# A delta-rule recurrence with two feed-forward blocks: one product's queue, two merged DMAs, masking from PSUM and a two-bank evacuation

## The chip, the cores and the metric

The kernel runs on one core of one Trainium2 chip. Times are device microseconds (us) of a whole execution. The engines are named as in the profile: PE is TensorE's matmul row and PEld its weight loads, DVE is VectorE, ACT is ScalarE, POOL is GpSimd, SP is the engine that here only issues DMAs. All arithmetic is fp32 or its two-part fp32r form.

## What is computed

Four batches, 8 heads, 768 steps, head size 40. Per batch and head a 40x40 state runs through all steps; its read-out y is then fed through two feed-forward blocks.

```python
for t in range(S):
    y[:, :, t] = np.einsum('bhd,bhde->bhe', rt, state)
    Sa = np.einsum('bhde,bhe->bhd', state, at)
    state_decay = state * wt[:, :, None, :] - np.einsum('bhd,bhe->bhde', Sa, bt)
    state = state_decay + np.einsum('bhd,bhe->bhde', vt, kt)
# y as (batch, step, head * dim) = x
x  = x + relu(layernorm(x) * g_ln @ w_ch1) @ w_ch2
h  = relu(x @ w_in)                       # then a 3-tap convolution along the steps
out = (h * sigmoid(conv(h))) @ w_out
```

## The kernel before

**Chunks.** The 768 steps are cut into 24 chunks of 32. Within a chunk the recurrence is turned into matrix products, so one chunk is a chain of five products, each followed by an evacuation from PSUM, and the chunk after needs its last one. `chunk` (L552) writes the chain for both halves of the batch (half 0 and 1): `st_re` makes `reps` on PE, and ACT copies it to `re`; `st_zh` (L480) makes `zhps` from `re` and a solved triangle `tm`, and DVE multiplies it by `zmask` into `r1` (L492, four instructions per half, one for each quarter of the partitions); `st_x` (L497) makes `xps`, from which DVE scales the next state into `r1` (L516, two per half) and ACT copies `yt` (the raw y); `st_s` transposes the state (`sps`, copied to `s` by ACT); `st_xr` makes `xrps`, which ACT copies into `r1`. Throwaway bf16 products on the identity (`burn`, L129) stand ahead of some of these, three ahead of each `zhps`.

**Groups.** Two chunks are a group G (12 of them). `stage` prepares a group some 8 to 10 chunks ahead: loads, decays (the products of w, on DVE for the first four groups, then on POOL), the scaled k, b, a, their transposes (`tr`), and for each of its two chunks `inner` (L388): PE makes the 16 products `aps`, ACT writes minus them to SBUF (`pst`, L402), and DVE multiplies `pst` by `nmask`, minus a triangular mask, into the operand `l1` (L413, four instructions a chunk, eight a group). After the second chunk of the group two DMAs on SP store half of `pst` to DRAM (`pd`, L407).

**Solve.** Two groups are a quartet of four chunks, Q. `solve` (L419) loads their `pd` transposed into `sv` (L424, one buffer), inverts 128 unit triangles by 30 pairs of multiply and add (L431 and L433; on DVE for quartet 0, on POOL for the others), and stores them (`td`, L434). `load_tm` (L437) loads them back for each group, four DMAs, as `tm`, which `st_zh` needs.

**Side work.** `side` puts the following group's operands beside each chunk: `gmat` (`gps`, masked by DVE at L460), `load_stacks` (r from v at L226, l from ks at L229), and `yout` (L561), which transposes a quarter of an earlier quartet's `yt` (`yps`), multiplies it on DVE by the decays `gtok` (L575, one instruction for each half), and stores each half with a DMA of its own (L578) to `xs`, a DRAM tile for each batch and half of the steps. `load_g` (L370) loads `gtok` once a quartet with four DMAs, one for each batch (L372).

**PSUM.** Three pools of two buffers: `pm`, one bank a buffer (`reps`, `zhps`, `sps`, `xrps` in turn), `px`, two banks a buffer (`xps`), and `pside`, one bank a buffer (`tr`, `tre`, `aps`, `gps`, `yps`).

**Order.** The program gives each instruction a priority by chunk (`at`), and a list scheduler places every engine's instructions in one fixed order from these and its own model of durations; on the chip each engine keeps that order. Waits follow from the tiles.

**After the recurrence** the feed-forward blocks run over eight blocks of 384 steps; `load` (L883) reads a block of `xs`. Their code is not touched but for that index.

## Time and profile before

| | us |
|---|---|
| runs before, median (three runs, 940.84 to 951.85) | 951.68 |
| the profiled execution | 944.43 |
| its span, first to last instruction | 942.7 |
| busy in the span: PE, DVE, ACT, POOL | 820.1, 679.3, 513.7, 273.6 |

The span has three parts: the start-up up to the first `zhps` product, the 24 chunks, and the feed-forward blocks. A busy share says which engine has much to do, not which wait ends last; on this kernel the latter is read from the gaps in PE and DVE within a chunk. Times in the rows count from the span's start.

### The profile page before, as it was taken

Reading aid. Unit: us, or ns where it says so; the run is one execution under the profiler, and the core shown is the slowest. Engines: PE = TensorE matmul, PEld = TensorE weight load, DVE = VectorE, ACT = ScalarE, POOL = GpSimd, SP = SyncE. Lnnn points to the kernel's source line nnn. Section 1 sums busy time; section 2 is a strip of 40 time slices with the busy share of each in tenths; the row PEclk is TensorE's granted clock in tenths of the full one; section 3 lists DMA queues with packets and bytes.
Section 4 is the critical chain, followed back from the end, with each engine's and each line's share of the span. In section 5 each row is a group of like instructions: output and inputs, shape, how many; then the busy total and the mean of one; then the engine's idle time right before and its main releaser. Section 6 shows DMA issues by size and latency. Waiting matters only on the chain.

```text
span 942.7 us, 24879 instructions
## 1 busy us (share of the span) xinstructions
PE 820.1 (87%) x9959; PEld 721.8 (77%) x9959; DVE 679.3 (72%) x1646; ACT 513.7 (54%) x1166; POOL 273.6 (29%) x498
## 2 busy tenths in 40 slices
PE   0575587797989999979998898999999999999996
PEld 0454465675767777757767877999999999999996
DVE  8879848677667786779888989785649482756356
ACT  6267255854766766545544357564438362746354
POOL 9403268359339448085112222000000000000000
PEclk9867798997999999998999989999999999999999
DMA  5997784684697585683745541101010000000000
GB/s 153 206 235 193 185 170 97 170 186 98 170 166 182 149 164 110 133 158 91 145 109 153 142 114 50 36 1 36 1 36 15 22 15 2 29 1 15 15 15 32
DMA packets 218544, 94.21 MB, mean 100 GB/s; under 512 B 176860, under 2 KB 207924, under 8 KB 218420
## 3 DMA queue, kind: packets, MB, share of 16 engines
q1 hardware_dynamic: 217524, 90.24, 40.8%
q0 software_dynamic: 896, 2.30, 1.1%
q8 instruction: 80, 1.31, 0.6%
q14 instruction: 44, 0.36, 0.1%
HBM read 63.78 MB, written 28.72 MB: 98 GB/s over the span
## 4 chain that ended last, share of the span: by engine, by line
PE 49%; DVE 20%; DMA 8%; ACT 5%; POOL 4%; issue 3%; SPq 2%; DVEq 0%; ACTq 0%; POOLq 0%
PE ups L946 17%; PE acc L956 9%; PE accb L956 8%; DVE r L492 4%; PE xps L505 3%; DVE l L413 3%; PE tps L924 2%; PE tr L323 2%; POOL sv L433 2%; POOL svt L431 1%; PE xrps L544 1%; PE aps L397 1%; DMA x<-xs 1%; DVE r L460 1%; PE reps L474 1%
## 5 line engine op out<-in xcount | busy, mean ns | idle before, releaser
L492 DVE TENSOR_TENSOR r<-zhps,zmask 32x288 f32<-32x288 f32 x192 | 87.2, 454 | 33.7 <-PE zhps L487 28.1
L964 DVE SCALAR_TENSOR_TENSOR rl<-ups,rh 128x384 fp32r<-128x384 f32 x80 | 44.6, 557 | 82.6 <-ACT rh L963 82.4
L963 ACT ACTIVATE rh<-ups 128x384 fp32r<-128x384 f32 x80 | 39.0, 490 | 105.7 <-PE ups L946 105.1
L505 PE MATMUL xps<-r,l 128*40 128x72 f32 x1536 | 82.0, 239 | 13.2 <-DVE r L492 12.3
L505 PEld LDWEIGHTS xps<-r,l 128*40 128x40 f32 x1536 | 62.7, 122 | 32.8 <-DVE r L492 24.9
L433 POOL TENSOR_TENSOR sv<-sv,svt 128x30 f32<-128x30 f32 (+9 forms) x150 | 83.3, 555 | 9.4
L946 PE MATMUL ups<-xh,w1h 128*128 128x384 f32 x240 | 81.2, 339 | 1.7 <-DVE rl L964 1.3
L431 POOL TENSOR_TENSOR svt<-sv 128x30 f32<-128x30 f32 (+9 forms) x150 | 77.9, 520 | 9.2
L946 PE MATMUL ups<-xh,w1l 128*128 128x384 f32 x240 | 80.6, 336 | 0.0
L413 DVE TENSOR_TENSOR l<-pst,nmask 32x256 f32<-32x256 f32 x96 | 58.3, 607 | 24.5 <-ACT pst L402 23.4
L956 PE MATMUL acc<-w2h,rh 128*128 128x320 f32 x240 | 71.6, 310 | 1.7 <-ACT rh L963 1.7
L956 PE MATMUL acc<-w2l,rh 128*128 128x320 f32 x240 | 71.4, 307 | 0.0
L946 PE MATMUL ups<-xh,w3l 128*128 128x384 f32 x192 | 65.1, 341 | 0.3 <-POOL w3l L806 0.3
L134 ACT COPY yt<-xps 40x256 f32<-40x256 f32 x96 | 35.2, 367 | 55.0 <-DVE r L516 50.5
L946 PE MATMUL ups<-xh,w3h 128*128 128x384 f32 x192 | 64.4, 342 | 0.6 <-ACT h L988 0.4
L956 PE MATMUL accb<-w4h,ph 128*128 128x320 f32 x192 | 59.1, 313 | 0.0
L956 PE MATMUL accb<-w4l,ph 128*128 128x320 f32 x192 | 58.7, 309 | 0.0
L956 PE MATMUL acc<-w2h,rl 128*128 128x320 f32 x240 | 49.8, 312 | 6.0 <-DVE rl L964 6.0
L956 PE MATMUL accb<-w4h,pl 128*128 128x320 f32 x192 | 53.4, 311 | 0.6 <-DVE pl L1010 0.6
L946 PE MATMUL ups<-xl,w1h 128*128 128x384 f32 x160 | 53.5, 335 | 0.0
L999 DVE SCALAR_TENSOR_TENSOR c<-h,taps,c 128x256 f32<-128x256 f32 (+1 forms) x88 | 43.9, 508 | 12.8 <-ACT c L997 12.6
L516 DVE TENSOR_TENSOR r<-xps,ge 40x320 f32<-40x320 f32 x96 | 46.7, 486 | 8.3 <-PE xps L505 6.1
(190 smaller groups left out, 2219.4 us busy)
## 6 DMA issues: line engine op xcount, KB each, us to landing
l<-ks SPq DMA_DIRECT2D x44, 160.0 KB, 3.5
raw<-in_moe_w_ch_dram SPq DMA_DIRECT2D x17, 320.0 KB, 3.4
ks<-p_b SPq DMA_DIRECT2D x12, 416.0 KB, 3.3
ks<-p_k SPq DMA_DIRECT2D x12, 416.0 KB, 4.0
ld_w<-in_w_dram SPq DMA_DIRECT2D x24, 160.0 KB, 3.3
ld_k<-in_k_dram SPq DMA_DIRECT2D x24, 160.0 KB, 4.2
ld_a<-in_a_dram SPq DMA_DIRECT2D x24, 160.0 KB, 3.7
ld_b<-in_b_dram SPq DMA_DIRECT2D x24, 160.0 KB, 3.8
```

The source lines that it names most:

```text
L134: return self.nc.scalar.copy(out, in_).ins
L413: nc.vector.tensor_tensor(out=lv[v0:v0 + C, :, :, y, c, 32 * half:32 * half + C], in0=pst[64 * y:64 * y + C, :, :, half], in1=self.nmask[6 ...
L431: eng.tensor_tensor(out=tmp, in0=sv[:, 0:u, u:u + 1].to_broadcast([128, u, m]), in1=sv[:, u:u + 1, u + 1:C].to_broadcast([128, u, m]), op= ...
L433: last = eng.tensor_tensor(out=sv[:, 0:u, u + 1:C], in0=sv[:, 0:u, u + 1:C], in1=tmp, op=ALU.add)
L492: nc.vector.tensor_tensor(out=r1[z0:z0 + 32, :, x, MO[y]:MO[y] + 72], in0=ps[32 * q:32 * q + 32], in1=self.zmask[32 * q:32 * q + 32].rearr ...
L505: nc.tensor.matmul(ps[x0:x0 + D, j >> 2, o:o + 72], lhsT=l2[:, i, :], rhs=r1[:, j, MO[y]:MO[y] + 72], start=True, stop=True)
L516: last = nc.vector.tensor_tensor(out=r2[X0:X0 + D, :, :, VO[y]:VO[y] + D], in0=pv[x0:x0 + D, :, :, v:v + D], in1=ge[X0:X0 + D, :, :, y, c: ...
L946: self.mm = self.nc.tensor.matmul(ps, lhsT=l, rhs=r, start=(i == 0), stop=(i == len(passes) - 1)).ins
L956: self.mm = self.nc.tensor.matmul(acc[n][:, 0:DM], lhsT=l, rhs=r, start=(f == 0 and i == 0), stop=(f == nf - 1 and i == 2)).ins
L963: nc.scalar.activation(rh, ps, AF.Relu)
L964: nc.vector.scalar_tensor_tensor(out=rl, in0=ps, scalar=0.0, in1=rh, op0=ALU.max, op1=ALU.subtract)
L999: nc.vector.scalar_tensor_tensor(out=c, in0=h(1), scalar=w(1), in1=c, op0=ALU.mult, op1=ALU.add)
```

## The change

- The two halves swap their partitions (`XR0`, `VR0`, `ZR0`), so that half 0 stands first in `yt`; batch indices follow.
- `nmask` goes. L413 now reads the product in PSUM and multiplies by `mask` instead of reading `pst` and multiplying by `nmask`. ACT still writes `pst`, for the store.
- The `pd` stores are issued by ACT instead of SP.
- `gtok` is loaded with one DMA a quartet instead of four.
- `yout` multiplies both halves in one instruction and stores both with one DMA. For that `xs` becomes one DRAM tile for each half of the steps that holds all batches.
- `zhps` moves from `pm` to `px`. Its products for the two row groups (x = 0, 1) go to partitions 0 to 63 of two banks instead of to the two halves of the partitions of one bank, and two instructions of 576 columns a half replace four of 288 at L492.

```diff
     def st_zh(self, n, half, re):
-        r1 = self.r1[n % 2][half].rearrange("p (k x) m -> p k x m", x=2)
-        ps = self.psm("zhps")[:, 0:288].rearrange("p (k m) -> p k m", k=4)
+        r1 = self.r1[n % 2][half].rearrange("p (k x) m -> p x k m", x=2)
+        ps = self.psx("zhps")[0:64, :, 0:288].rearrange("p x (k m) -> p x k m", k=4)
...
-            nc.tensor.matmul(ps[64 * x:64 * x + 64, k, :], lhsT=tm[64 * x:64 * x + 64, k, half, :],
+            nc.tensor.matmul(ps[:, x, k, :], lhsT=tm[64 * x:64 * x + 64, k, half, :],
...
-        for q in range(4):
-            x, y = q >> 1, q & 1
+        for y in range(2):
             nc.vector.tensor_tensor(
-                out=r1[z0:z0 + 32, :, x, MO[y]:MO[y] + 72], in0=ps[32 * q:32 * q + 32],
-                in1=self.zmask[32 * q:32 * q + 32].rearrange("p (o t) -> p o t", o=1).to_broadcast([C, 4, 72]),
+                out=r1[z0:z0 + 32, :, :, MO[y]:MO[y] + 72], in0=ps[32 * y:32 * y + 32],
+                in1=self.zmask[32 * y:32 * y + 32].rearrange("p (o q t) -> p o q t", o=1, q=1).to_broadcast([C, 2, 4, 72]),
                 op=ALU.mult)
```

```diff
     def inner(self, n):
...
-            for y in range(2):
-                nc.sync.dma_start(out=self.pd[n // 4][:, 64 * g + 32 * y:64 * g + 32 * y + 32],
-                                  in_=self.pst[64 * y + 32:64 * y + 64].rearrange("s x c k f t -> s (x c k f) t"))
+            self.pd_store(self.pd[n // 4][:, 64 * g:64 * g + 64])
...
+        pv = ps.rearrange("p (k x) (f t) -> p x k f t", x=2, f=2)
...
-                    in0=pst[64 * y:64 * y + C, :, :, half],
-                    in1=self.nmask[64 * y:64 * y + C].rearrange("p (o q t) -> p o q t", o=1, q=1).to_broadcast(
+                    in0=pv[64 * y:64 * y + C, :, :, half],
+                    in1=self.mask[64 * y:64 * y + C].rearrange("p (o q t) -> p o q t", o=1, q=1).to_broadcast(
...
+    def pd_store(self, pd):
+        for y in range(2):
+            self.nc.scalar.dma_start(out=pd[:, 32 * y:32 * y + 32],
+                                     in_=self.pst[64 * y + 32:64 * y + 64].rearrange("s x c k f t -> s (x c k f) t"))
```

```diff
     def load_g(self, Q):
-        for b in range(B):
-            self.nc.sync.dma_start(out=self.gtok[:, b], in_=self.gs[Q][b].rearrange("h t e -> t h e"))
+        self.nc.sync.dma_start(out=self.gtok.rearrange("t b h e -> t (b h) e"),
+                               in_=self.gs[Q].rearrange("b h t e -> t (b h) e"))
...
     def yout(self, Q, part):
-        for half in range(2):
-            ys = self.tile([128, 4, D], f"ys_{half}", YB, self.yp)
...
+        ys = self.tile([128, 2, 4, D], "ys", YB, self.yp)
...
+        nc.sync.dma_start(out=self.xs[Q // 3][b01::2, t0:t0 + 128, D * h0:D * h0 + 4 * D].rearrange("b t e -> t b e"),
+                          in_=ys.rearrange("p b h e -> p b (h e)"))
```

## Rows read from the trace of the kernel before

**Rows 1.** Engines' busy time by stretch (instructions in brackets), granted TensorE clock, DMA share

```profile
0.00:113.00 113.00, 56.58 (x598) 44.07 (x599) 93.93 (x259) 61.07 (x109) 47.81 (x75) 0.79 0.79 198
113.00:188.00 75.00, 59.39 (x1166) 46.78 (x1166) 48.56 (x86) 45.28 (x100) 42.70 (x91) 0.89 0.64 144
188.00:259.00 71.00, 63.30 (x1208) 49.50 (x1209) 50.87 (x99) 42.60 (x97) 43.20 (x88) 0.89 0.66 151
...
502.00:943.00 441.00, 419.25 (x2612) 409.92 (x2611) 299.50 (x799) 221.22 (x534) 23.07 (x28) 0.99 0.13 36
```

**Rows 2.** DVE's timeline in chunk 14: start, us, instructions merged

```profile
356.16 6.32 DVE L413 TENSOR_TENSOR l<-pst,nmask 32x256 f32<-32x256 f32 x8 [2.17 <-ACT pst L402]
362.51 0.56 DVE L575 TENSOR_TENSOR ys<-yps,gtok 128x160 f32<-128x160 f32 x2
363.10 3.85 DVE L492 TENSOR_TENSOR r<-zhps,zmask 32x288 f32<-32x288 f32 x8
...
368.29 2.00 DVE L516 TENSOR_TENSOR r<-xps,ge 40x320 f32<-40x320 f32 x4
```

**Rows 3.** PE's timeline in chunk 14

```profile
357.73 0.71 PE L474 MATMUL reps<-r,l 128*32 128x72 f32 x32
...
360.73 0.72 PE L487 MATMUL zhps<-re,tm 64*64 64x72 f32 x16
```

**Rows 4.** Groups of instructions by line: busy us, mean ns | idle before

```profile
L413 DVE TENSOR_TENSOR l<-pst,nmask 32x256 f32<-32x256 f32 x96 | 58.3, 607 | 24.5 <-ACT pst L402 23.4
```

**Rows 5.** Durations of single instructions, min/median/max ns, by tile

```profile
L492 DVE TENSOR_TENSOR r<-zhps,zmask x192: 446/453/465, 115.0 to 500.5; 32x288 f32<-32x288 f32 x192
...
L516 DVE TENSOR_TENSOR r<-xps,ge x96: 450/484/495, 120.5 to 502.6; 40x320 f32<-40x320 f32 x96
...
L413 DVE TENSOR_TENSOR l<-pst,nmask x96: 404/416/4919, 40.3 to 394.6; 32x256 f32<-32x256 f32 x96
L407 SPq DMA_DIRECT2D pd<-pst x24: 319/422/1616, 46.0 to 392.3; - x24
```

**Rows 6.** DVE's timeline around chunk 6

```profile
216.28 9.73 DVE L413 TENSOR_TENSOR l<-pst,nmask 32x256 f32<-32x256 f32 x8 [3.58 <-ACT pst L402]
```

**Rows 7.** PE's timeline around chunk 6

```profile
220.32 0.72 PE L487 MATMUL zhps<-re,tm 64*64 64x72 f32 x16
...
227.12 0.46 PE L505 MATMUL xps<-r,l 128*40 128x72 f32 x2 [5.74 <-DVE r L492]
```

**Rows 8.** DVE's timeline in chunk 2

```profile
142.40 10.35 DVE L413 TENSOR_TENSOR l<-pst,nmask 32x256 f32<-32x256 f32 x8 [3.69 <-ACT pst L402]
```

**Rows 9.** PE's timeline in chunk 2

```profile
146.76 0.72 PE L487 MATMUL zhps<-re,tm 64*64 64x72 f32 x16
154.19 1.10 PE L323 MATMUL tr<-ident,p_a 128*104 128x128 f32 x4 [6.71 <-DVE r L460]
```

**Rows 10.** Waits over the whole span: us in total, times, longest

```profile
ACT yt L134 <- DVE r L516: 50.5, 16, 13.6
...
PEld tr L323 <- DVE r L460: 8.8, 3, 6.9
PE zhps L487 <- DMA tm<-td: 8.6, 5, 3.9
```

**Rows 11.** PE's timeline, the first `zhps` of chunks 4 and 8

```profile
188.51 0.71 PE L487 MATMUL zhps<-re,tm 64*64 64x72 f32 x4 [3.10 <-DMA tm<-td]
...
260.44 0.68 PE L487 MATMUL zhps<-re,tm 64*64 64x72 f32 x14 [1.22 <-DMA tm<-td]
```

**Rows 12.** SP's timeline between two solves

```profile
326.89 2.08 SPq L407 DMA_DIRECT2D pd<-pst  x2
...
331.21 4.38 SPq L372 DMA_DIRECT2D gtok<-gs  x4
335.64 0.75 SPq L424 DMA_DIRECT2D sv<-pd  x1
```

**Rows 13.** Issue of the `sv` load, min/median/max ns

```profile
L424 SPq DMA_DIRECT2D sv<-pd x6: 387/496/752, 59.1 to 396.2; - x6
```

More of the change, by code (lines that the diff above doesn't have):

```diff
@@ L20 @@
 NQ = NCH // 4
-XR0 = (64, 0)
-VR0 = (0, 64)
-ZR0 = (32, 96)
+XR0 = (0, 64)
+VR0 = (64, 0)
+ZR0 = (96, 32)
 SLOT = 168
@@ L89, in __init__ @@
         self.kb = T([128, 16, 2, 64], "kb", ep)
-        self.mask, self.nmask = T([128, C], "mask"), T([128, C], "nmask")
+        self.mask = T([128, C], "mask")
         self.zmask = T([128, 72], "zmask")
@@ L120, in psm, with psx @@
         return self.burn(self.pm.tile([128, 512], F32, tag="m", name=name), BURN.get(name, 0))
-    def psx(self):
-        ps = self.px.tile([128, 2, 512], F32, tag="x", name="xps")
-        self.burn(ps[:, 0], BURN.get("xps", 0))
+    def psx(self, name="xps"):
+        ps = self.px.tile([128, 2, 512], F32, tag="x", name=name)
+        self.burn(ps[:, 0], BURN.get(name, 0))
         return ps
@@ L166, in constants @@
         P.memset(self.kb[96:128], 0.0)
-        V.tensor_scalar(self.nmask, self.mask, -1.0, None, op0=ALU.mult)
         self.at(-16.5)
@@ L572, in yout @@
         pv = ps[:, 0:416].rearrange("p (h m) -> p h m", h=4)
-        for half in range(2):
-            ys = self.tile([128, 4, D], f"ys_{half}", YB, self.yp)
-            self.last_out = nc.vector.tensor_tensor(
-                out=ys, in0=pv[:, :, XR0[half]:XR0[half] + D], in1=self.gtok[:, 2 * half + b01, h0:h0 + 4],
-                op=ALU.mult).ins
-            nc.sync.dma_start(out=self.xs[2 * half + b01][Q // 3][t0:t0 + 128, D * h0:D * h0 + 4 * D],
-                              in_=ys.rearrange("p h e -> p (h e)"))
+        ys = self.tile([128, 2, 4, D], "ys", YB, self.yp)
+        self.last_out = nc.vector.tensor_tensor(
+            out=ys, in0=bass.AP(tensor=pv.tensor, offset=pv.offset, ap=[pv.ap[0], [64, 2], pv.ap[1], [1, D]]),
+            in1=self.gtok[:, b01::2, h0:h0 + 4], op=ALU.mult).ins
+        nc.sync.dma_start(out=self.xs[Q // 3][b01::2, t0:t0 + 128, D * h0:D * h0 + 4 * D].rearrange("b t e -> t b e"),
+                          in_=ys.rearrange("p b h e -> p b (h e)"))
     def at(self, t):
@@ L1167, in sequential @@
             for i in range(B):
-                nc.sync.dma_start(out=xs[i][half][bass.ds(t0, step), :].rearrange("t (h e) -> h t e", h=H),
+                nc.sync.dma_start(out=xs[half][i][bass.ds(t0, step), :].rearrange("t (h e) -> h t e", h=H),
                                   in_=y[H * i:H * i + H])
@@ L1181, in run_kernel @@
         excess = cp.tile([128, 2 * NG], F32, name="excess")
-        xs = [[dp.tile([TG, DM], F32, name=f"xs_{i}{j}") for j in range(2)] for i in range(B)]
+        xs = [dp.tile([B, TG, DM], F32, name=f"xs_{j}") for j in range(2)]
         early = ExitStack()
```

10 lines of the change are left out of this document (5 added, 5 removed).

## The prediction

> **What bounds the kernel now.** I read the stretches first. [rows 1] cut the span at the first `zhps` (113 us) and after the last chunk (502 us): a start-up of 113, a recurrence of 389, and 441 for the feed-forward blocks, where PE is busy 419 of 441. The change touches nothing in the last part but the shape of `xs`, so whatever it does must be found in the first 502 us, and above all in the 389 of the chunks, 16.2 us a chunk. In the two stretches of [rows 1] between 113 and 259 PE is busy 59.4 of 75 and 63.3 of 71: there is room, but no engine is full.
>
> Second, one chunk on DVE and PE. In chunk 14 [rows 2] DVE runs without a pause from 356.16 to 370.3: masking (L413) 6.32, then the eight `zhps` evacuations 3.85, then a mask of side work, then the state (L516) 2.00. The `zhps` product of half 0 was ready at 360.73 + 0.72 = 361.45 [rows 3], and its evacuation began at 363.10, behind the masking. So here DVE's queue sets the pace, and the masking is what stands in the way.
>
> Third, the masking itself. L413's median is 416 ns, its longest 4919 [rows 5]; 96 of them take 58.3 us [rows 4], where 96 medians would be 39.9. The surplus of 18.4 sits in a few groups of eight, which should take 8 x 0.416 = 3.3: 10.35 in chunk 2 [rows 8], 9.73 around chunk 6 [rows 6], 6.32 in chunk 14 [rows 2], that is 7.0, 6.4 and 3.0, and 2.0 elsewhere. The instructions that read PSUM and a mask in SBUF never show this: L492 446 to 465, L516 450 to 495 over the whole recurrence [rows 5]. L413 is the one of them with both sources in SBUF. In chunk 6 the harm is plain: the second `zhps` ended at 221.04, and PE's next stall of 5.74 us ended at 227.12 with L492 [rows 7]. In chunk 2 PE stood 6.71 us, from 147.48 to 154.19, before a `tr` that needed the bank masked at L460, and L460 was queued behind L413 [rows 8, 9].
>
> Fourth, what stands beside the chunks. The `tm` of every fourth chunk comes from the solve: PE waited 3.10 us for it in chunk 4 and 1.22 in chunk 8 [rows 11], 8.6 in five waits in all [rows 10]. So the loop pst, `pd`, `sv`, solve, `td`, `tm` is as long as four chunks to within a few us: it is late next wherever a chunk gets shorter.
>
> **The change part by part.** The sum is made against the profiled execution, 944.4 us (span 942.7).
>
> *Masking from PSUM.* No row shows 256 columns from PSUM. L492 takes 453 for 288 and L516 484 for 320 [rows 5], about 1 ns a column, so 256 take about 0.42 us: as fast as L413's median, but without the stalls. DVE saves 96 x (0.607 - 0.422) = 17.8 us. On the path I count what PE or the evacuation waited: 6.7 in chunk 2, 5.7 in chunk 6 and 363.10 - 361.45 = 1.6 in chunk 14, together 14. Bounds: 0, if the solve gives all back, and 17.8.
>
> It does not spare the wait for `pst`. L413 waited 23.4 us for ACT's `pst` [rows 4], and would seem to need only the product now. But ACT's `yt` copies waited 50.5 us for DVE's L516 [rows 10], though both only read `xps`: readers of one PSUM tile on two engines are put one behind the other, and `pst` is written first. [...]
>
> *The price of that.* A bank of `aps` is now free only after its four masks (1.7 us) instead of after `pst`, and the two chunks of a group hold both `pside` banks together for up to 3.4 us, in which no `tr`, `gps` or `yps` can start. The cover is the chain, which uses the other pools. The nearest row is L460, which holds a bank in the same way: `tr` waited 8.8 us for it, 6.9 of it once [rows 10], in chunk 2 behind the stalled masking, so 1.9 without a stall. Eight groups fall in the recurrence: 0 to 8 x 3.4 = 27. A static order made with that holding in view will move side work away; I take 0.4 each, 3 us, near the row's 1.9.
>
> *z and H in two instructions.* An instruction of 576 columns should cost 0.453 + 288 x 0.97 ns = 0.73 us, against 0.91 for two of 288 [rows 5]. Eight with their gaps take 3.85 [rows 2]; four will take about 3.85 - 4 x 0.17 - 4 x 0.03 = 3.05. So 0.8 us a chunk, 19 over 24 chunks, is the upper bound. The first `xps` products used to start after the first two of four evacuations and can no longer, so of half 0's share little reaches the path. I take 0.6 a chunk, 14 us. Lower bound 0.
>
> *The products for it.* The two row groups now write the same partitions in two banks. The trace never shows two row groups on one set of columns. Bounds: 16 records took 0.72 us in two column groups and 32 in 0.71 in four [rows 3]; less about 0.22 for the first, 33 and 16 ns a record, so four groups run twice as fast as two and one group would need 66: (0.72 - 0.22) x 2 + 0.22 = 1.22, or 0.5 more a half, 48 x 0.5 = 24 us. Lower bound 0, which I take: row groups are separate parts of the array as column groups are, and every row here has groups running beside each other. [...]
>
> `zhps` in `px` has to wait for the readers of the last chunk's `xps`, L516 and the `yt` copies; L516 ends at 370.3 [rows 2], while the next `zhps` is due a chunk of 16.2 us after 360.73 [rows 3], near 377, so nothing.
>
> *pd on ACT's queue.* An issue takes 0.42 us in the median and 0.59 in the mean (14.2 for 24), 0.32 at least [rows 5]. 16 of the 24 fall in the recurrence: 16 x 0.42 = 6.7, to 9.4, of ACT's time right after `pst`, with `re`, `r` and `s` copies queued behind it. About a third should meet a copy that is waiting: 3 us. SP loses the same issues: in [rows 12] two of them took 2.08 directly on the way to the next solve.
>
> *gtok in one DMA, y in one store.* Four `gtok` issues took 4.38 us just ahead of an `sv` load [rows 12]; that `sv` load has as many short pieces as a merged one and is issued in 0.50 [rows 13]. SP gets free 3.9 us earlier, but the bytes are the same and `sv` follows them, so I take half, 2, and with `pd` 1 more: 3 us less on a solve loop where this order occurs. `yout`: 0.56 for two [rows 2] becomes about 0.48; 24 x 0.08 = 2, off the path. The loss of `nmask` is one small instruction.
>
> **The sum.** Gains of the chunks: 14 + 14 = 28. But the solve paces too. Up to chunk 4 the chunks gain 6.7 + 4 x 0.6 = 9.1, while PE already waits 3.10 there: only what the solve itself gains, about 2 from SP and a POOL that DVE's masking no longer disturbs, comes through. At chunk 8 the same: 2 more, of 8.1. From there on PE does not wait as much, the earlier masking starts the third solve earlier, and the chunks' own gain can come through: 3 for chunks 8 to 11, 4 for 12 to 15 with the stall of chunk 14, 2.4 each for 16 to 19 and 20 to 23. Together 2 + 2 + 3 + 4 + 2.4 + 2.4 = 15.8. Less 3 for ACT's issues and 3 for the held banks: 9.8. 944.4 - 9.8 = 934.6. The profiled execution is 7.3 below the median of the runs shown, and these spread over 11 us; the same share, 1.04%, off 951.68 gives 941.8. I put the median of the changed kernel between the two, at 938.0, which is 1.4% under the median shown.
>
> **The rivals.**
>
> *The chunks' gain comes through whole* (chance 0.27). For it: the masking's stalls are direct waits of PE, and once chunk 6 is quick the third solve starts sooner; the solve loop contains SP issues of 2.08 and 4.38 that go. Also PE's granted clock is 0.89 from 113 to 259 [rows 1], where the stalls are, so a steadier PE may get more of its higher level. Against: 3.10 and 1.22 us of waiting for `tm`. Time: 944.4 - 28 = 916 if the 3 from SP pay for ACT's issues, 919 with the held banks.
>
> *All is given back* (0.20). The solve loop is unchanged, each chunk 4Q waits for it, and the issues on ACT and held banks take the rest. Time: 944.4 - 2.4 (after the last solve) + 3 = 945.
>
> *Row groups on one set of columns do not run together* (0.10, the other side). The point from which it decides is a `zhps` group of 16 records longer than 0.72 + 15.8 / 48 = 1.05 us; at 1.22 it costs 24, and since `zhps` lies on the chain all of it counts: 934.6 + 24 = 959, slower than the profiled execution by 1.5%.
>
> *Held banks stop PE for their full length* (0.06): 27 in place of 3, 958.6.
>
> **How the numbers follow.** The forecast, with its own range of 928 to 944, has 0.37. A measurement of this kernel tells about 2% from no change: faster means below 932.6, slower above 970.7. Faster takes most of the first rival and a little of the forecast's lower end: 0.27. Slower needs two of the costs at once, or an order of the scheduler that nobody foresees: 0.10. The rest, 0.63, is no change. The range reaches from the first rival, 916, to the last two, 959, leaving out a tenth on each side.
>
> **What would show it.** L413's longest under 0.5 us and its 96 near 40: right on the stalls; still several us long: wrong. L492 96 instructions of 0.73 each, four in about 3.05. A `zhps` group still 0.72, else the third rival. PE's wait for `tm` should grow in chunks 4 and 8; if it does not and the last chunk ends before 485, the first rival holds. PE waiting for L413 or for `pst` with `tr`, `gps` or `yps` shows held banks. ACT copies late behind an issue of `pd` by more than 0.5 us each make the 3 us too small. What I can't see is the new static order, which can move any of this by several us.

## The result, and the profile after

The changed kernel takes 957.84 us (median of four, 957.3 to 958.2) where the kernel before, run beside it, takes 949.73: a ratio of 1.014, with a 95% interval of 1.010 to 1.018. A second comparison on another chip gives 953.86 against 941.9, again 1.014 (1.009 to 1.020). The ratios are estimates from all fast runs of both kernels and not quotients of these medians, which differ by 8.1 us, and on the second chip by 12.0. So it is slower by 8 to 13 us. That is inside the 2% that the forecast called no change and inside its range, but the forecast had its middle on the other side.

The spans of the two profiled executions differ by 13.1 us (955.8 and 942.7). The table cuts them at rows of PE's timeline: the first `aps` product, the first `zhps` of chunks 0, 16, 20 and 23, and the end. The third line is a second profile of the changed kernel.

| us | to first aps | to zhps 0 | chunks 0-16 | 16-20 | 20-23 | rest | span |
|---|---|---|---|---|---|---|---|
| before | 35.2 | 77.7 | 280.8 | 65.3 | 37.3 | 446.4 | 942.7 |
| after | 37.9 | 85.5 | 267.1 | 77.1 | 36.2 | 452.1 | 955.8 |
| after again | 34.8 | 84.9 | 266.7 | 74.3 | 36.5 | 450.1 | 947.3 |

The chunks up to the sixteenth did gain, 13.7 us. Three other places lost: 7.8 in the start-up behind the first `aps`, 11.8 in the four chunks 16 to 19, and 5.7 in the rest. In the second profile the gain is 14.1 and the losses are 7.2, 9.0 and 3.7. The 2.7 ahead of the first `aps` differ from one execution of the same kernel to the next.

First the parts that came out as written. Durations of single instructions of the kernel after (min/median/max ns, then first and last start), to be held against [rows 5]:

```profile
L411 DVE TENSOR_TENSOR l<-aps,mask x96: 405/418/423, 42.8 to 398.1; 32x256 f32<-32x256 f32 x96
...
L495 DVE TENSOR_TENSOR r<-zhps,zmask x96: 746/750/755, 125.0 to 506.8; 32x576 f32<-32x576 f32 x96
...
L420 ACTq DMA_DIRECT2D pd<-pst x24: 308/346/584, 45.2 to 394.8; - x24
```

The masking has no stall left: the longest of 96 is 423 ns, where it was 4919, and its 96 take 40.0 us for 58.3 [rows 4]. Four evacuations of z and H take 3.06 us for the eight's 3.85 [rows 2], as this row of DVE's timeline in chunk 2 shows:

```profile
152.99 3.06 DVE L495 TENSOR_TENSOR r<-zhps,zmask 32x576 f32<-32x576 f32 x4
```

Then the waits of the kernel after over the whole span (us in total, times, longest), beside [rows 10]:

```profile
PE zhps L491 <- DMA tm<-td: 15.9, 5, 9.7
...
PE tr L322 <- DVE l L411: 8.7, 5, 2.6
...
PE tre L322 <- DVE l L411: 8.2, 3, 4.7
...
PE ups L948 <- ACT w3h L806: 4.2, 3, 3.1
```

PE's wait for `tm` has nearly doubled, from 8.6. The two rows of L411 are the held banks: 16.9 us in which a transpose waited for the masking to free its bank. The last row is in the feed-forward part, where the kernel before waits 0.2 us.

The 9.7 us stand at one place, the first `zhps` of chunk 20, on PE's timeline:

```profile
467.56 0.71 PE L491 MATMUL zhps<-re,tm 64*64 64x72 f32 x4 [9.70 <-DMA tm<-td]
```

Its `reps` came at 454.4, two microseconds earlier than before's 456.4, but before went on with `zhps` at 459.0. What was late is the fifth of POOL's solves, that of quartet 5 for chunks 20 to 23; it is called the fifth solve here, and its way from `pd` to `tm` the fifth loop. SP's timeline where it begins, after and then before:

```profile
394.39 0.47 SPq L370 DMA_DIRECT2D gtok<-gs  x1
394.96 5.46 SPq L217 DMA_DIRECT2D ld_v<-in_v_dram  x1
400.52 1.03 SPq L225 DMA_DIRECT2D r<-in_v_dram  x2
...
404.87 1.26 SPq L428 DMA_DIRECT2D sv<-pd  x1
```

```profile
391.80 0.90 SPq L407 DMA_DIRECT2D pd<-pst  x2
396.16 0.39 SPq L424 DMA_DIRECT2D sv<-pd  x1
396.65 3.38 SPq L578 DMA_DIRECT2D xs<-ys  x2
400.08 3.55 SPq L372 DMA_DIRECT2D gtok<-gs  x4
```

Before, `sv` leaves 0.1 us after its `pd` landed at 396.1, and `gtok` follows it. After, `pd` lands at 399.7, and `sv` stands behind `gtok` and eight other loads: it leaves 5.1 us later, at 404.87. Once the solve runs, it takes 50.6 us on POOL (48.7 before), the longest of the five that POOL does, because POOL's fixed order, in both kernels, puts a weight subtraction between its pairs that waits for ACT (6.3 us here, 8.2 before):

```profile
438.07 0.62 POOL L437 TENSOR_TENSOR sv<-sv,svt 128x228 f32<-128x228 f32 x1
445.01 0.86 POOL L808 TENSOR_TENSOR w1l<-v,w1h 128x320 fp32r<-128x320 f32 x1 [6.32 <-ACT w1h L806]
```

In the second profile of the changed kernel this solve takes 47.6 us, less than before's 48.7, and chunk 20 still stands 11.8 us between `reps` and `zhps` (13.1 in the first profile, 2.6 before). So the solve's own length is not what was lost.

In the start-up `td` is late too, though its place in SP's queue is the old one. After, the solve on DVE ends at 109.7 and `td` leaves 5.0 us later, behind five other DMAs. Before, it ends at 103.5 and `td` leaves at 104.17, behind the same five, which had left by then. The first of them, `bd`, stores `blk`, a product of POOL, and that came later: 72.1 us behind the first `aps`, 64.7 before. The solve itself ended 3.4 us later, counted in the same way. The timelines of POOL and SP after, and then before:

```profile
109.62 0.35 POOL L235 TENSOR_TENSOR blk<-t 128x80 f32<-128x80 f32 x1
...
109.99 0.33 SPq L246 DMA_DIRECT2D bd<-blk  x1
111.54 0.58 SPq L248 DMA_DIRECT2D pre<-bd  x1
112.54 1.29 SPq L366 DMA_DIRECT2D gs<-p_g  x2
113.92 0.65 SPq L217 DMA_DIRECT2D ld_w<-in_w_dram  x1
114.66 0.54 SPq L438 DMA_DIRECT2D td<-sv  x1
```

```profile
99.47 0.35 POOL L236 TENSOR_TENSOR blk<-t 128x80 f32<-128x80 f32 x1
...
99.85 0.34 SPq L247 DMA_DIRECT2D bd<-blk  x1
...
104.17 0.64 SPq L434 DMA_DIRECT2D td<-sv  x1
```

### The profile page after: what moved, and what is told of

The parts are those of the page before. It is cut to its first block, busy times and chain, and to the rows that moved or that the text cites. A ratio compares the mean times of both kernels' runs of the same rounds, so it can differ in the third digit from the quotient of the medians.

```text
span 955.8 us, 24666 instructions
## 1 busy us (share of the span) xinstructions
PE 810.3 (85%) x9959; PEld 721.0 (75%) x9959; DVE 654.9 (69%) x1525; ACT 514.9 (54%) x1166; POOL 277.7 (29%) x498
## 4 chain that ended last, share of the span: by engine, by line
PE 47%; DVE 14%; DMA 8%; POOL 7%; ACT 5%; issue 4%; SPq 3%; DVEq 0%; ACTq 0%; POOLq 0%
PE ups L948 17%; PE acc L958 9%; PE accb L958 8%; POOL svt L435 3%; POOL sv L437 3%; DVE r L495 2%; PE xps L508 2%; DMA x<-xs 2%; PE tps L926 2%; DMA gtok<-gs 1%; PE xrps L547 1%; SPq L217 1%; PE zhps L491 1%; DVE r L519 1%; DVE p_k L286 1%
## 5 line engine op out<-in xcount | busy, mean ns | idle before, releaser
L495 DVE TENSOR_TENSOR r<-zhps,zmask 32x576 f32<-32x576 f32 x96 | 72.0, 750 | 38.7 <-PE zhps L491 36.9
L965 ACT ACTIVATE rh<-ups 128x384 fp32r<-128x384 f32 x80 | 39.1, 490 | 107.6 <-PE ups L948 107.3
L435 POOL TENSOR_TENSOR svt<-sv 128x30 f32<-128x30 f32 (+9 forms) x150 | 80.2, 535 | 9.9
L437 POOL TENSOR_TENSOR sv<-sv,svt 128x30 f32<-128x30 f32 (+9 forms) x150 | 80.2, 535 | 9.6
L508 PE MATMUL xps<-r,l 128*40 128x72 f32 x1536 | 64.9, 244 | 18.6 <-issue 11.4
L508 PEld LDWEIGHTS xps<-r,l 128*40 128x40 f32 x1536 | 57.4, 128 | 25.8 <-issue 12.9
L134 ACT COPY yt<-xps 40x256 f32<-40x256 f32 x96 | 35.2, 367 | 68.5 <-DVE r L519 67.4
L411 DVE TENSOR_TENSOR l<-aps,mask 32x256 f32<-32x256 f32 x96 | 40.0, 417 | 34.5 <-ACT pst L401 33.1
L491 PE MATMUL zhps<-re,tm 64*64 64x72 f32 x768 | 37.9, 240 | 19.5 <-DMA tm<-td 15.9
L519 DVE TENSOR_TENSOR r<-xps,ge 40x320 f32<-40x320 f32 x96 | 46.8, 487 | 10.1 <-PE xps L508 8.5
```

The lines of the kernel that those rows point to most:

```text
L134: return self.nc.scalar.copy(out, in_).ins
L411: nc.vector.tensor_tensor(out=lv[v0:v0 + C, :, :, y, c, 32 * half:32 * half + C], in0=pv[64 * y:64 * y + C, :, :, half], in1=self.mask[64 ...
L435: eng.tensor_tensor(out=tmp, in0=sv[:, 0:u, u:u + 1].to_broadcast([128, u, m]), in1=sv[:, u:u + 1, u + 1:C].to_broadcast([128, u, m]), op= ...
L437: last = eng.tensor_tensor(out=sv[:, 0:u, u + 1:C], in0=sv[:, 0:u, u + 1:C], in1=tmp, op=ALU.add)
L491: nc.tensor.matmul(ps[:, x, k, :], lhsT=tm[64 * x:64 * x + 64, k, half, :], rhs=re[64 * x:64 * x + 64, k, :], start=True, stop=True)
L495: nc.vector.tensor_tensor(out=r1[z0:z0 + 32, :, :, MO[y]:MO[y] + 72], in0=ps[32 * y:32 * y + 32], in1=self.zmask[32 * y:32 * y + 32].rearr ...
```

## The experiments

All ratios are to the kernel before, run beside each on the same chip. The tables give stretches as above, from each run's profile.

### One part taken back at a time

Theories: Q, the fifth `sv` is late because it stands behind `gtok`; H, the banks held by the masking delay the fifth `pd`; S, the loss is spread by the new order; Z, `zhps` in `px` waits for readers.

**gtok behind sv.** `load_g` is ordered behind the last `sv` load on SP.

```diff
-            self.load_g(n // 4)
+            with self.tc.issue_after(self.sv_load):
+                self.load_g(n // 4)
```

> The changed kernel with one order forced: each gtok load is issued after the latest sv load (they share SP's queue). Theory Q (the one-piece gtok load fills SP's queue ahead of the fifth sv load, so the fifth solve comes late): PE's 9.70 us wait for tm at the first zhps of chunk 20 falls under 2 us, the fifth sv load is issued at its pd's landing instead of 5 us later, and the time falls by 7 to 9 us, to about 949. Theory H (the masks hold both pside banks and so delay the solve's input): the wait stays above 6 us and the time within 3 us of 957.8. Theory S (any new order moves the start and the tail by several us): the time may fall or rise by up to 10 us, with the chunk 20 wait not the place of it.

**gtok in four loads again.**

```diff
-        self.nc.sync.dma_start(out=self.gtok.rearrange("t b h e -> t (b h) e"), ...)
+        for b in range(B):
+            self.nc.sync.dma_start(out=self.gtok[:, b], in_=self.gs[Q][b].rearrange("h t e -> t h e"))
```

> The changed kernel with gtok loaded by four DMAs again; the order still has the fifth sv load seven places behind it. Theory Q in its first form (one big DMA blocks, four small ones do not): the issue right behind gtok falls from 5.46 us to under 2, the chunk 20 wait to under 5, time about 952. Theory Q in its second form (the bytes ahead of sv count, not the number of issues): four issues take 3.5 to 4.4 us together as in the kernel before, the wait stays at 8 to 10 us, time 956 to 959. Theory H: 957.8 within 3.

**Masks from SBUF again.**

```diff
-                    in0=pv[64 * y:64 * y + C, :, :, half],
-                    in1=self.mask[64 * y:64 * y + C]...
+                    in0=pst[64 * y:64 * y + C, :, :, half],
+                    in1=self.nmask[64 * y:64 * y + C]...
```

> The changed kernel with L413's masking from pst and nmask in SBUF again, everything else as changed. Theory H: the held banks were the loss; tre and tr no longer wait for masks, time 945 to 950. [...] Theory S: anything between 945 and 965.

**z and H in one bank again**, four instructions a half.

```diff
-        ps = self.psx("zhps")[0:64, :, 0:288].rearrange("p x (k m) -> p x k m", k=4)
+        ps = self.psm("zhps")[:, 0:288].rearrange("p (k m) -> p k m", k=4)
...
-        for y in range(2):
+        for q in range(4):
+            x, y = q >> 1, q & 1
```

> The changed kernel with zhps in one bank of pm and four evacuations of 288 a half again. In its order the fifth sv load stands six places ahead of gtok. Theory Q: no wait over 2 us at chunk 20, which gives 8 back; the chunks lose 0.6 each, 14 over the recurrence where nothing else paces; time 952 to 960, with the first zhps still after 120 us. Theory Z (moving zhps into px cost the time, since its products wait for the copies of yt): time 944 to 950 and xps no longer waiting.

| | ratio (95%) | first aps to zhps 0 | 0-16 | 16-20 | rest |
|---|---|---|---|---|---|
| after | 1.014 (1.010-1.018) | 85.5 | 267.1 | 77.1 | 452.1 |
| gtok behind sv | 1.011 (1.002-1.020) | 80.4 | 268.8 | 77.5 | 450.0 |
| gtok in four | 1.015 (1.005-1.024) | 85.8 | 268.0 | 76.2 | 452.6 |
| masks from SBUF | 1.015 (1.006-1.023) | 79.3 | 276.2 | 74.6 | 450.8 |
| z, H in one bank | 1.015 (1.005-1.024) | 85.6 | 277.8 | 74.4 | 448.9 |

Taking back the masking or the evacuation costs the chunks 0 to 16 9.1 and 10.7 us. But no single undoing brings back the 65.3 of chunks 16 to 19. With `gtok` behind `sv`, `sv` left at once, but `pd` itself landed 14.8 us after chunk 16's `zhps` instead of 9.2: Q alone is not it. With `gtok` in four, `sv` left 6.8 us after its `pd`: the number of DMAs is not it. With the masks from SBUF the banks are free again and the wait stays, so H alone is not it either. Z finds little: the throwaway products ahead of `zhps` wait 1.2 us in all for the copies of `yt` in the changed kernel, and at most 4.0 in any version here. What remains is S, that the order as a whole is another one, and that is not yet a mechanism.

### Each part alone, and the solve halved

Theory L: the loop of `pd`, `sv`, solve, `td` and `tm` takes the chunks' gain back. M: the start-up is lost by the masking from PSUM. Rivals are named in the expectations.

**Masks from PSUM alone**, on the kernel before.

```diff
-                    in0=pst[64 * y:64 * y + C, :, :, half],
-                    in1=self.nmask[64 * y:64 * y + C]...
+                    in0=pv[64 * y:64 * y + C, :, :, half],
+                    in1=self.mask[64 * y:64 * y + C]...
```

> Kernel before with one part alone: masks read PSUM and nmask goes. Theory M (the lost start-up comes with masking from PSUM): first zhps near 123 us as in the changed kernel (112.9 before), chunks 0 to 16 about 9 us quicker than before's 280.8, so near 272, and the time about that of the kernel before or up to 8 us more, ratio 1.000 to 1.008. Rival P (the start-up was lost by pd on ACT's queue or the one gtok load): first zhps near 113, and then the time is below before's by up to 5 us. Theory L (the loop of the solve takes the chunks' gain back at chunk 20): PE waits 5 to 10 us for tm at chunk 20 (0 before).

**z and H in two banks alone**, the `st_zh` of the change on the kernel before.

```diff
-        ps = self.psm("zhps")[:, 0:288].rearrange("p (k m) -> p k m", k=4)
+        ps = self.psx("zhps")[0:64, :, 0:288].rearrange("p x (k m) -> p x k m", k=4)
```

> Kernel before with one part alone: zhps in two banks of px, two evacuations of 576 columns a half. Start-up untouched: first zhps near 113. Chunks 0 to 16 about 10 us quicker than 280.8, near 271. Theory L (solve loop): PE waits at chunk 20 for tm, 5 us or more, and the time is below before's by no more than 5 us, ratio 0.995 to 1.000. Rival K (the loss at chunk 20 comes from the masks' holding of pside or from the store and load order of the other parts): no wait at chunk 20, and the whole 10 us stay, ratio 0.989.

**Half of solves 1 to 5 left out**, in the kernel before and in the changed one. Both leave out every second pair of multiply and add on POOL, so they compute something else and serve for their times only.

```diff
-        for u in range(C - 2, 0, -1):
+        for u in range(C - 2, 0, -1 if eng is nc.vector else -2):
```

> Kernel before, but solves 1 to 5 (on POOL) do only every second pair of multiply and add, so td holds other numbers; each solve is some 20 us shorter. This is the base for the next run. By theory L the kernel before waits 8.6 us for tm in all, and these go: 5 to 12 us less than before. Rival N (the solve is hidden in the kernel before): within 3 us of it.

> Changed kernel with the same half of solves 1 to 5 left out. Theory L (solve loop takes the chunks' gain back): the wait of 9.7 us at chunk 20 is gone, so it is quicker than the changed kernel by 12 us or more, and compared with the kernel before with the same half left out the stretch from first zhps to the end of chunk 23 is 12 to 18 us shorter, the start-up 10 us longer: the two within 5 us of each other, before side by side 13 apart. Rival K (chunk 20 waits for something else): the wait stays within 3 us and so does the distance of 13 us to the base.

**pd on ACT's queue alone.**

```diff
-                nc.sync.dma_start(out=self.pd[n // 4]...
+                nc.scalar.dma_start(out=self.pd[n // 4]...
```

> Kernel before with one part alone: pd is issued by ACT. By the prediction's term 3 us are lost on ACT and 1 gained on SP: ratio 1.000 to 1.004, no wait at chunk 20. Rival O (any change of the order of SP around the fifth solve starts it late, whatever the part): sv of the fifth solve leaves 5 us or more after its pd landed, PE waits 8 us or more at chunk 20, ratio 1.008 to 1.015.

**gtok in one load and y in one store alone**, with the swap of the halves that they need.

```diff
-        for half in range(2):
-            ys = self.tile([128, 4, D], f"ys_{half}", YB, self.yp)
+        ys = self.tile([128, 2, 4, D], "ys", YB, self.yp)
...
-        for b in range(B):
-            self.nc.sync.dma_start(out=self.gtok[:, b], ...)
+        self.nc.sync.dma_start(out=self.gtok.rearrange("t b h e -> t (b h) e"), ...)
```

> Kernel before with gtok in one load, y of both halves in one multiply and one store (with the swap of the halves), all else as before. By the prediction's term at most 3 us less. Rival O (any other order on SP loses the fifth loop): sv leaves late behind gtok, 16 to 20 takes 73 to 78 (65.3 before), ratio 1.008 to 1.015. If the tail after the chunks is 440 or more (436 before), the 5 us that the changed kernel loses there come from the merged y store.

| | ratio (95%) | first aps to zhps 0 | 0-16 | 16-20 | rest |
|---|---|---|---|---|---|
| before | | 77.7 | 280.8 | 65.3 | 446.4 |
| masks alone | 1.015 (1.007-1.024) | 81.8 | 271.7 | 78.0 | 447.7 |
| z, H alone | 1.022 (1.015-1.030) | 79.8 | 278.4 | 77.8 | 447.5 |
| pd on ACT alone | 1.010 (1.005-1.014) | 78.9 | 273.7 | 76.3 | 445.0 |
| gtok and y alone | 1.023 (1.017-1.029) | 78.9 | 276.1 | 79.5 | 453.3 |
| before, half solve | 0.989 (0.985-0.993) | 80.1 | 266.6 | 65.4 | 446.3 |
| after, half solve | 0.986 (0.978-0.994) | 86.0 | 250.3 | 67.2 | 450.2 |

Four quite different edits lose the same 11 to 14 us in chunks 16 to 19, and together they lose no more. So it is not something that a part costs; it is something that the order of the kernel before has and the orders of these four lack. The granted clock does not go with it: in these chunks it was 0.92 before, 0.88 after, and 0.93 with `pd` on ACT alone, which lost 11.0. The row of `pd` on ACT alone, PE's timeline at chunk 20:

```profile
469.61 0.74 PE L487 MATMUL zhps<-re,tm 64*64 64x72 f32 x4 [6.15 <-DMA tm<-td]
```

The times missed what was expected of three of the four: the masks alone 1.015 for at most 1.008, z and H alone 1.022 for at most 1.000, `gtok` and y alone 1.023 for at most 1.015. `pd` on ACT came out in its rival's range, but not by the rival's way: `sv` left 1.2 us after its `pd` had landed, where 5 or more were named.

The half solve says what takes the gain. The kernel before gets 1.1% quicker by it; the changed kernel, 1.4% above before with a whole solve, ends 1.4% below, and the chunks 16 to 19 are back at 67.2. In this execution chunk 20 goes from `reps` to `zhps` without a stop:

```profile
436.21 0.71 PE L478 MATMUL reps<-r,l 128*32 128x72 f32 x32
436.85 0.72 PE L491 MATMUL zhps<-re,tm 64*64 64x72 f32 x16
```

PE waits for `tm` no longer at all (15.9 us with the whole solve; the base falls from 8.6 to 4.1). With the solve out of the way the chunks from 0 to 23 take 355.8 us, 15.3 below the base's 371.1, where with the whole solve they take 380.4, 3.0 below before's 383.4. So the loop of the solve takes back 12.3 of 15.3. That is theory L. The half solve gives the base more than a shorter loop, though: its 96 masks, both of whose sources lie in SBUF, take 48.8 us for 58.3, while POOL has less to do. So 15.3 may be less than the parts are worth without a loop. The two were expected within 5 us of each other; the changed kernel came out 4.6 below.

M holds in part: the masks alone lose 4.1 us behind the first `aps`, and taking them back from the changed kernel returns 6.2; the other parts alone lose 1.2 to 2.1, no more than the kernel before with half the solve (2.4). The late `blk` goes with the masks: where the start-up's masks read SBUF, it ended 64.7 to 66.5 us behind the first `aps` in all eleven profiles, and where they read PSUM 70.5 to 73.3 in seven of eight. The eighth is `gtok` behind `sv`: there `blk` ended at 58.3, `td` left as the solve ended, and 5.1 us came back with the masks still in PSUM. So in the first profile 4.3 of the 7.8 us are `td` held behind a `bd` that waits for POOL, and most of the others the solve's later end; why the masks put POOL and the solve late was not moved alone.

The rest of the loss, 5.7 us (3.7 in the second profile), goes with the y of both halves in one store: `gtok` and y alone have 453.3 us behind the chunks; the twelve profiles with the merged store have 447.3 to 453.3, the seven without it 444.8 to 447.7. `gtok` in four did not mend it (452.6). In `gtok` and y alone PE's `ups` waits 4.2 us for `w3h`, as in the changed kernel. Which of SP's loads holds `w3h` up was not tried. Part of the loss can be PE's clock: behind the chunks PE is busy 424.3 us at a granted clock of 0.99 before, 425.9 at 0.98 in the changed kernel, and 428.7 at 0.97 in `gtok` and y alone. But in the second profile of the changed kernel it is 423.3 at 0.99, and 3.7 are lost all the same.

### What in the fifth loop is late

Theory O: SP's fixed order puts `sv`, `td` and `tm` of the fifth solve behind other DMAs.

**The w1l subtractions kept on DVE until chunk 21** (`SUBN = 21` for 18), so that POOL's fifth solve waits for nothing; on the kernel before, on the changed kernel, and on the changed kernel with the start-up's masks from SBUF.

> Kernel before, with the subtractions that make w1l kept on DVE until chunk 21 (POOL takes them from chunk 18), so that the fifth solve on POOL does not wait for ACT's w1h (8.2 us in the kernel before). Base for the next run. The kernel before does not wait at chunk 20, so by theory L (solve loop) this brings it little: within 3 us, ratio 0.997 to 1.003. Rival T (the subtractions on DVE cost as much as they free): 3 to 8 us slower.

> Changed kernel with the same edit. Theory L: the fifth solve falls from 50.5 us to about 40, PE's wait at chunk 20 from 13 us between reps and zhps to 2 to 5, and the time by 8 to 11 against the changed kernel, so to a ratio of 1.002 to 1.006. Rival G (the chunk-20 loss comes from the late store and load of the fifth pd and not from the length of the solve): the wait stays above 8 and the time within 4 us.

> The same edit, and the masks of the first four groups (start-up) read pst in SBUF as in the kernel before, the rest PSUM. If the start-up is lost by masking from PSUM (held banks, and the order that follows), from the first aps to the first zhps goes from 85.5 back to 78 to 80 us and the time is another 5 to 8 us below the run before it: ratio 0.993 to 0.999 to the kernel before. Rival: the start-up stays at 85 us and the time within 2 us of the run before it.

**The fifth loop first on SP.** On the last of these, the loads of chunks 20 and 21 are ordered behind `td`, and `gtok` and the weights of chunk 19 behind the first four `tm` loads; then behind all eight.

```diff
+        with self.tc.issue_after(self.tml) if n == 19 else ExitStack():
+            ws.step(NOTH)
...
+            with self.tc.issue_after({15: self.svl, 19: self.tml}[n]) if n in (15, 19) else ExitStack():
+                self.load_g(n // 4)
...
+            with self.tc.issue_after(self.tds) if n in (18, 19) else ExitStack():
+                self.load_stacks(n + 2)
```

> The kernel of e11 (changed kernel, w1l on DVE until chunk 21, start-up masks from SBUF), and on SP the fifth solve's sv, td and first tm stand ahead of gtok, of the weight loads of chunk 19 and of the loads of chunks 20 and 21. Theory L with O (the fifth loop is long because SP's fixed order puts its DMAs behind others): td leaves within 1 us of the solve's end (6.3 in e11), its tm within 1 us of td's landing, PE's wait at chunk 20 falls from 7.7 between reps and zhps to 2 to 4, the stretch 16 to 20 from 73.7 to 64 to 68, and the time by 5 to 8 us, ratio 1.001 to 1.005. Rival D (the solve itself and the late pd set it): 16 to 20 stays above 72 and the time within 2 us of e11.

> The kernel of e13, and the fifth solve's second tm too stands ahead of gtok and of the weight loads on SP (in e13 it left at 459.2 behind gtok, and chunk 22 came 18.3 us after chunk 21). Theory L with O: chunks 20 to 23 fall from 41.1 to 36 to 37, 16 to 20 stays at 69 or less, ratio 1.000 to 1.004. Rival D: the wait moves again, to the tail or to another chunk, and the time stays where e13 was, ratio 1.006 to 1.010.

**Only the parts that shorten chunks**, on the kernel before: z and H in two banks, and the masks of the fifth group on from PSUM, with w1l on DVE and the first of these orders for the fifth loop.

```diff
-                    in0=pst[64 * y:64 * y + C, :, :, half],
+                    in0=(pst if n < 8 else pv)[64 * y:64 * y + C, :, :, half],
```

> Kernel before with only those parts that shortened the chunks: zhps in two banks, masks from PSUM from the fifth group on; with w1l on DVE until chunk 21 and the same order on SP for the fifth loop. pd on SP, gtok in four and y in two stores as before. Theory L with O: start-up 78 to 80 from the first aps, chunks 0 to 16 about 268, 16 to 20 about 66, the tail as before's 436: 10 to 14 below the kernel before, ratio 0.985 to 0.990. Rival D: the loop takes the gain back elsewhere, ratio 0.997 or more.

**The changed kernel once more**, beside the last but one.

> The changed kernel once more, beside the last. Theory L with O: it is 10 us or more slower than e16, from the start-up (6 us from the first aps to the first zhps) and chunks 16 to 20 (77 against 69). Theory S2 (the first aps begins at 33 us in some executions and at 38 to 41 in others of one and the same kernel): the profile may show another begin of aps than 37.9, while 85.5 from there to the first zhps stays.

The steps of the fifth loop, from the rows of DMAs and POOL in each profile (us):

| | pd lands after zhps 16 | sv leaves after that | solve | td after its end | first tm after td | reps 20 to zhps 20 | ratio (95%) |
|---|---|---|---|---|---|---|---|
| before | 2.4 | 0.1 | 48.7 | 0.0 | 3.1 | 2.6 | |
| after | 9.2 | 5.1 | 50.6 | 0.0 | 2.6 | 13.1 | 1.014 |
| pd on ACT alone | 11.1 | 1.2 | 48.2 | 0.0 | 5.1 | 9.7 | 1.010 |
| w1l on DVE, before | 2.8 | 0.1 | 41.0 | 5.2 | 5.6 | 2.6 | 0.998 (0.994-1.002) |
| w1l on DVE, after | 9.4 | 5.2 | 40.6 | 7.2 | 4.4 | 12.6 | 1.013 (1.009-1.018) |
| and start-up masks from SBUF | 11.8 | 0.1 | 39.3 | 6.3 | 3.6 | 7.7 | 1.010 (1.006-1.014) |
| and loop first on SP | 12.7 | 0.1 | 40.3 | 0.0 | 4.3 | 2.5 | 1.008 (1.004-1.012) |
| and all tm first | 12.3 | 0.1 | 39.1 | 0.0 | 3.6 | 2.2 | 1.004 (1.000-1.008) |

The second experiment missed by all of its 10 us, and that is the most telling line. POOL's solve did fall by 10.0 us, and nothing came of it, since `td` stood behind other DMAs until SP got to it. SP's timeline of that kernel; the solve had ended at 457.2:

```profile
457.92 0.61 SPq L580 DMA_DIRECT2D xs<-ys  x1
458.58 1.56 SPq L370 DMA_DIRECT2D gtok<-gs  x1
460.50 3.88 SPq L780 DMA_DIRECT2D raw<-in_moe_w_ch_dram  x3
464.47 0.54 SPq L438 DMA_DIRECT2D td<-sv  x1
```

The third got the 6 us of the start-up that were expected (79.0 for 85.2), but it is at 1.010 where 0.993 to 0.999 was named: its chunks 0 to 16 took 273.2 us for 269.9.

With the loop first on SP, `td` leaves at the solve's end, 441.5, and the wait at chunk 20 is gone. In the first form of it (1.008, where 1.001 to 1.005 was expected) the wait moved on by two chunks: the second four `tm` loads still stood behind `gtok`, and chunk 22 came 18.3 us after chunk 21.

```profile
441.53 0.33 SPq L440 DMA_DIRECT2D td<-sv  x1
...
445.85 2.00 SPq L450 DMA_DIRECT2D tm<-td  x4
...
458.64 0.47 SPq L372 DMA_DIRECT2D gtok<-gs  x1
459.15 6.69 SPq L450 DMA_DIRECT2D tm<-td  x4
```

With all eight ahead, chunks 20 to 23 take 34.6 us for 41.1, and the kernel is at 946.0 against the changed kernel's 953.86 on the same chip, 7.9 less, where 10 or more was expected. These 7.9 hold three edits: w1l on DVE, the start-up's masks and SP's order. The order alone is the step from the third version to the last: 1.010 to 1.004, with intervals that overlap, the wait at chunk 20 from 7.7 to 2.2 us between `reps` and `zhps`, and chunks 16 to 23 from 112.6 us to 105.2. So theory O is shown for the wait that is left once the solve is 10 us shorter; with the solve at its old length the order was not tried. It is not the whole of it. The fifth `pd` still lands 12.3 us after chunk 16's `zhps`, and chunks 16 to 19 take 70.6 and not 65.3. Why every order but before's makes that `pd` so late is open: in the traces the last product of the last group's `aps` ends 4.2 us ahead of chunk 16's `zhps` in the kernel before (and in it with w1l on DVE), and 0.4 us ahead to 10.6 behind it in the others, but no run moved it alone.

The kernel with only the chunks' parts missed too: 1.013 (1.009 to 1.016). There the fifth loop was in order (2.1 us at chunk 20), but chunk 8 stood 14.8 us between `reps` and `zhps`, for the loop of quartet 2. The loss had moved to another quartet, as theory L allows and its expectation, with 268 us for the chunks to the sixteenth, did not: they took 277.6. Chunks 16 to 19 took 73.2 us, where 66 was expected, and not for `tm`: DVE stood 4.5 and 2.6 us for `gtok`, which this order had put behind an `sv` that left only at 406.2. The first of the two on DVE's timeline:

```profile
413.34 0.32 DVE L575 TENSOR_TENSOR ys<-yps,gtok 128x160 f32<-128x160 f32 x1 [4.45 <-DMA gtok<-gs]
```

So putting the loop first has a price of its own. No version here that does the whole solve beats the kernel before by more than its interval; the nearest is before with w1l on DVE, 0.998 (0.994 to 1.002).

## Why the prediction was wrong, step by step

**The stalls of the masking: right.** The 96 take 40.0 us, as the 0.42 us each said. What the stalls stood beside the prediction did not name: POOL ran its solve in all the long ones (10.35, 9.73, 5.57 and 6.32 us for eight masks; where POOL ran no solve, eight took 3.5 at most), and with half of the solve left out the same 96 took 48.8 us for 58.3. That the masks are not spared the wait for `pst` came out as said: 33.1 us in ten waits, where it was 23.4 in eight. And ACT's `yt` copies wait 67.4 us for L519, where they waited 50.5 for L516: in both kernels they stand behind DVE's reading of the same tile. Taking the part back costs 9.1 in chunks 0 to 16, where 14 were put on the path; alone it gave 9.1 too, but with a stop of 14.2 us between `reps` and `zhps` at chunk 12 (3.0 before), so that the two agree by chance.

**z and H: the instruction right, its share of the path not settled.** 0.75 us an instruction for the 0.73 estimated, 3.06 for 3.05 a chunk. Taken back, the part costs 10.7 us in sixteen chunks, 0.67 a chunk for the 0.6 taken; alone it gave 2.4, with 6.8 us of waiting for `tm` at chunk 12. PE's `xps` waits for the evacuation 1.5 us in all, where it was 12.3. `pd` on ACT, which shortens no chunk, gave 7.1 alone, so a new order by itself moves this stretch by several us, and the sizes of single parts are no finer than that.

**Two row groups on the same columns: right at 0.** The 16 records still take 0.72 us (at 359.84 in the profile of the changed kernel, and in the rows of chunk 20 above), and the shortest single one 222 ns, both as before. That is 33 ns a record behind the first, where one group at a time was put at 66, so the rival of serial groups falls. That two row groups run beside each other on one set of columns, in two banks, is shown by this 0.72 alone; ahead of it the 0 was the author's estimate.

**Held banks: right in place, larger in the waits.** They were put at 3 us on the path; PE's transposes waited 16.9 us for L411. The chunks up to the sixteenth gained all the same, so the rival of 27 us on the path falls; how much of the 16.9 lay on the chain no run shows.

**ACT's issues: right to be small.** 24 issues of 0.35 us; the trace puts one wait of ACT, 3.5 us, down to a `pd` store.

**Chunks 0 to 16: the total near, its places not.** The sum gave 2 + 2 + 3 + 4 = 11 for them, less most of the 6 for ACT and the banks; they gained 13.7. But by quartets they gained 8.5, 5.4 and 0.3, and then lost 0.5. The first of these began 10.5 us later in the span, and its gain did not make up for that: chunk 4's first `zhps` came at 190.5, where it had come at 188.5 [rows 11]. The sign named for the loop, a longer wait at chunks 4 and 8, did not show either: 6.9 and 2.1 us stood between `reps` and `zhps` there, for 9.1 and 3.0 before. PE's granted clock in these chunks rose from 0.93 to 0.96, so part of the gain may be the clock's, as the first rival had allowed. That the total comes near is luck.

**The loop of the solve: the step that failed.** The prediction saw that the loop is as long as four chunks and took its own length as given, or 3 us shorter by what SP gets free. It let 2.4 us come through for chunks 16 to 19. They lost 11.8, and 9.0 in the second profile, with PE waiting 9.7 us for `tm` at chunk 20. Three terms were wrong there. The gain from `gtok` was not there: one issue takes 0.47 us, but the next DMA on SP then takes 5.46 (the rows of SP above), 5.9 in all with some 0.6 of that load's own (0.58 in the median before), for the four's 4.38 [rows 12]. The place of `sv` and `td` in SP's order was taken from before's rows, where `sv` leaves at once; a new static order put them behind other DMAs, 5.1 us for `sv` at the fifth solve. And `pd` came 6.8 us later against the chunk, the largest of the three, whose cause stays open. Nor did POOL gain much from the shorter masks: a multiply of 128x240 takes 0.62 us, where it took 0.68 beside the mask of chunk 2, but the 300 multiplies and adds of its five solves 160.4 us for 161.2. The rival in which all is given back had the mechanism, at 0.20, but it held the loop at its old length, so that its time of 945 was the worst that it allowed. The half solve shows that the loop is what decided: with it the chunks gain 15.3, with the whole solve 3.0. The 28 of the first rival are not there even so, and that 15.3 is near the sum's 15.8 is chance, since those were to come through with the whole solve.

**The start-up: left out of the sum.** "Above all in the 389 of the chunks" was said of a change that also moves SP's queue and the banks in the start-up. There the solve on DVE is a bare chain of `pd`, `sv`, solve, `td`, `tm` with no cover, and 7.8 us were lost on it, 4.3 of them by `td` behind the late `blk`.

**The feed-forward part: not untouched.** It lost 5.7 us, 3.7 in the second profile. They go with the merged store; that it is SP's order behind the chunks is not shown.

**The chances.** Slower had 0.10 for "an order of the scheduler that nobody foresees". The measured 1.4% is inside the 2% that counted as no change, but a mechanism that four parts alone all meet was not a matter of one in ten. And the range reached up to 959 for two costs that did not come, serial row groups and banks held in full; that it holds 957.84 is luck.

## What to carry to other kernels

Where a list scheduler places every queue afresh, a local gain has to be checked against the longest loop that it shortens, and each hop of that loop (its store, load, result store and reload) against what else its queue issues around it. When the traces show a loop just hidden behind the work, as here with waits of 1 to 4 us, first free the loop, by ordering its DMAs ahead of the others, and only then make the work shorter. That this pays is not shown here: the one version that did so for a single loop moved the loss to another. A part whose cost alone is larger than that of all parts together points to the order and not to the part.

## What the runs showed of the hardware

**A copy within SBUF took 5.48 us beside POOL's memsets, and 0.48 ahead of them.** In the start-up DVE copies 40x640 from SBUF to SBUF while POOL fills SBUF. Two executions of the changed kernel, DVE's timeline and POOL's, first the one whose first `aps` began at 37.9:

```profile
17.21 0.48 DVE L187 COPY l<-ident 40x640 f32<-40x640 f32 x1
...
18.12 5.48 DVE L187 COPY l<-ident 40x640 f32<-40x640 f32 x1
...
23.80 3.19 DVE L187 COPY l<-ident 40x640 f32<-40x640 f32 x1
```

```profile
17.96 5.30 POOL L199 MEMSET l<- 128x2048 f32 x3
```

and the one that began at 34.8:

```profile
18.28 1.50 DVE L187 COPY l<-ident 40x640 f32<-40x640 f32 x1
...
20.20 1.67 DVE L187 COPY l<-ident 40x640 f32<-40x640 f32 x1
...
22.06 1.90 DVE L187 COPY l<-ident 40x640 f32<-40x640 f32 x1
```

The same copy takes 0.48 us ahead of the memsets, and 5.48 where three of them follow each other. In the second execution POOL's three took 6.20, from 17.41 on, and each of three copies beside them 1.50 to 1.90. The four copies of this kind take 9.6 us in the first and 5.6 in the second, and the first `aps` lies 3.1 apart, though no run shows that the copies alone moved it; in all profiled kernels it began anywhere from 32.9 to 40.7. What holds a copy up, and why it took 5.48 in one execution and 1.50 in the other, these rows do not show.

**The DMA behind a `gtok` in one load took 5.46 us on SP.** Where a `gtok` of 640 KB, by its shape 4096 rows of 160 bytes, is issued in 0.47 us and another DMA follows at once on SP, that one takes long: 5.46 (`ld_v`) above, where the median of such a load is 0.58 before, and 6.69 with three more behind it (`tm`), where the four `tm` ahead of that `gtok` took 2.00. Where the `gtok` itself took 1.56, the three behind it took 3.88 (`raw`). The issue row of this `gtok` alone, 0.47, does not show the time that SP spent behind it.
